# Position bias of an attention and mixture kernel: units decided on whole distances in float16, against knots computed once

## The chip, the cores and the metric

The kernel runs on one core of a Trainium2 chip. The metric is the time of one execution on the device, in microseconds (us). The engines of a core run side by side, each through its own list of instructions in order: TensorE (PE; PEld is its weight loads), VectorE (DVE), ScalarE (ACT), GpSimd (POOL), and SyncE (SP), which here issues DMA transfers. SBUF is the core's working memory, PSUM the memory into which TensorE's products go.

## The reference

Three blocks follow each other: an attention with a learned position bias (batch 2, 8 heads, 576 positions, 64 wide), a three-way max block, and eight experts over which a gate spreads 1152 tokens. The change is in the position bias alone:

```python
rel = (pos[:, None] - pos[None, :]).astype(np.float32)
psi_rel = np.log1p(np.abs(rel))
psi_i = np.log1p(np.maximum(pos[:, None].astype(np.float32), 1.0))
x = (psi_rel / psi_i)[..., None]
h = np.maximum(x @ w1 + b1, 0.0)        # 32 hidden units
bias = h @ w2                           # 8 heads
scores = scores + bias.transpose(2, 0, 1)[None, :, :, :]
```

A hidden unit d is active for row i and column j where w1[d] * psi_rel + b1[d] * psi_i is positive. Where it is active it adds w1[d] * w2[d, h] to a sum A and b1[d] * w2[d, h] to a sum B, and the bias is A * psi_rel / psi_i + B.

## The kernel before

The rows i are taken in 36 blocks of 16 (`g16`), and each block in four groups of 4 rows (`g`, 144 in all). For a group, `gen_s` makes a tile `s` of 128 partitions (4 rows by 32 units) and 576 columns that tells by sign which units are active. It compares a window of the table `lw` (logarithms of distances, times w1, float32), which moves by 4 columns from group to group, with a threshold per partition. ScalarE does this with a sign function (1 or -1) in 58 groups, VectorE with a comparison less one half (0.5 or -0.5, line 282) in 86; `ON_DVE` says which. Since these values are not 1 and 0, a constant is added back: A's in the bias of line 339, B's by a product of `cb` with `sel` (line 332).

`bias_mm` sums over the units on TensorE: for a block 32 products of 288 columns, with block-diagonal weights `wb` in two float16 parts, into PSUM tiles for A and for B; a 128-wide result holds 16 rows by 8 heads. `bias_ev` takes A out of PSUM on ScalarE (`t`, line 339) and multiplies it by the logarithms on GpSimd (line 342; on VectorE in the last two blocks, `LASTV`). `bias_out` joins it with B on VectorE (`bo`, line 347) and writes it to DRAM, from where the heads load it later.

The order is written out by hand. For each block come its products, `bias_ev`, the four `gen_s` of the block two later, and `bias_out`; in every other block GpSimd also prepares a sixth of a piece of the first head's operands (`prep_head`, lines 61 and 190). Buffers: 12 tiles `s`, 2 PSUM tiles each for A and B, 2 tiles `t`, 4 tiles `bo`. Ahead of the loop stand the loads of parameters (`par`) and tables, 12 products that nobody reads, and the weights' scaling on VectorE (lines 244 to 272). Behind the loop the attention starts with line 427 on VectorE and line 438 (exponentials) on ScalarE.

Of the kernel before, what the change touches and what calls it, by code (L numbers as in the profile page):

```python
# [27 lines left out]
SH = S // 2  # L28
# [14 lines left out]
ON_DVE = (0, 2, 4, 6, 8, 10, 11, 13, 14, 16, 18, 19)  # L43
ITS = [(0, 128), (128, 128), (256, 128), (384, 128), (512, 64)]

# [5 lines left out]
def make_body(stop=None):  # L51
    def body(tc, a):
# [21 lines left out]
        with ctx, tc.manual_schedule():  # L74
# [16 lines left out]
            def prep_w64(r, hi, lo):  # L91
                """A float64 weight tile [128, 512], made float32 on its bits and split, in steps."""
# [4 lines left out]
                # the exponent's floor is where float32's lowest exponent, and so 0, is made  # L97
# [25 lines left out]
            def w_step(n=1, last=99):  # L123
                """The next n steps of the weights' preparation, up to an item."""
# [15 lines left out]
            # ------------------------------------------------ operands of the heads  # L140
# [25 lines left out]
            def prep_head(h, k, part=None):  # L166
                """Operands of head h, piece k: hi, then what is left."""
# [34 lines left out]
            # ------------------------------------------------ position bias  # L202
            with ExitStack() as bctx:
# [5 lines left out]
                lw = bc.tile([128, L4_W], F32, name="lw")  # L209
                tab16 = bc.tile([128, L16_W + NG16], F32, name="tab16")  # L210
                dma(par, a["par"])
                # of the windows that slide over the logarithms, the first ones are the rightmost
                cuts = (0, 476, L4_W)
                nc.scalar.dma_start(out=lw[:, cuts[1]:], in_=a["tab4"][:, cuts[1]:])
                dma(lw[:, :cuts[1]], a["tab4"][:, :cuts[1]])
# [5 lines left out]
                # products that nobody reads, to have the tensor engine's clock up when the data are there  # L221
# [6 lines left out]
                half = bc.tile([32, 96], F32, name="half")  # L228
                G.memset(half, 0.5)
                sel = bc.tile([96, SH], BF16, name="sel")  # L230
                G.memset(sel, 0.0)
                for p in range(3):
                    G.memset(sel[32 * p:32 * p + 1], 1.0)
                bcv = bc.tile([128, NG4], F32, name="bcv")
                thr = bc.tile([128, NG4], F32, name="thr")
                pool_scale(bcv, c4, b1r)
                pool_copy(thr, bcv, -1.0)
                for sl in (slice(cuts[1], None), slice(0, cuts[1])):
                    A.activation(out=lw[:, sl], in_=lw[:, sl], func=AF.Identity, scale=w1r)
                # the power of two that brings the weights' largest product under 2^14, and its inverse  # L240
# [16 lines left out]
                # times 8, as the scores get their 1/8 with the bias in them  # L257
# [4 lines left out]
                # block-diagonal weights: [half-weights?, A or B, (i4, h)], in two float16 parts  # L262
                wf = bc.tile([128, 2, 2, 32], F32, name="wf")
                for q in range(2):
                    V.tensor_tensor(
                        out=wf[:, 0, q, :].rearrange("p (i h) -> p i h", h=H),
                        in0=ab[:, q, :].unsqueeze(1).to_broadcast([128, 4, H]),
                        in1=msk.rearrange("p (i h) -> p i h", h=H), op=ALU.mult)
                V.tensor_scalar(out=wf[:, 1], in0=wf[:, 0], scalar1=0.5, scalar2=None, op0=ALU.mult)
                wb = [bc.tile([128, 2, 2, 32], F16, name=f"wb{p}") for p in range(2)]  # L270
                V.tensor_copy(out=wb[0], in_=wf)
                V.tensor_tensor(out=wb[1], in0=wf, in1=wb[0], op=ALU.subtract)
                s_t = {}

                def gen_s(g):
                    s = sp.tile([128, S], F16, tag="s", name="s")
                    win = lw[:, L4_OFF - 4 * g:L4_OFF - 4 * g + S]
                    on_act = g % 20 not in ON_DVE
                    if on_act:
                        A.activation(out=s, in_=win, func=AF.Sign, bias=bcv[:, g:g + 1])  # L280
                    else:
                        V.tensor_scalar(out=s, in0=win, scalar1=thr[:, g:g + 1], scalar2=0.5,  # L282
                                        op0=ALU.is_gt, op1=ALU.subtract)
                    s_t[g] = s, int(on_act)
# [3 lines left out]
                # the constant part of the sums, by half-weights: A's with the row's logarithm, and B's as a  # L288
                # product of three bf16 parts (32 rows each) with ones in one row of each part
                ab16 = bc.tile([32, 2, 16, H], F32, name="ab16")  # L290
                for q in range(2):
                    G.tensor_copy(out=ab16[:, q], in_=ab[:32, q, :].unsqueeze(1).to_broadcast([32, 16, H]))
                cb = bc.tile([96, 128], BF16, name="cb")
                cr = bc.tile([96, 128], F32, name="cr")
                aic = bc.tile([128, 1 + 2 * NG16], F32, name="aic")
                a0, ia0, ics = aic[:, 0:1], aic[:, 1:1 + NG16], aic[:, 1 + NG16:]

                rows = ab16.rearrange("k q i h -> k q (i h)")
                T.matmul(out=p0[:, 0, 0:1], lhsT=rows[:, 0], rhs=half[:, 0:1], start=True, stop=True)
                T.matmul(out=p0[0:96, 0, 128:256], lhsT=half, rhs=rows[:, 1], start=True, stop=True)  # L300

                def consts():
                    V.tensor_scalar(out=ics, in0=ic16, scalar1=sc[:, 1:2], scalar2=None, op0=ALU.mult)
                    V.tensor_copy(out=a0, in_=p0[:, 0, 0:1])
                    V.tensor_scalar(out=ia0, in0=ics, scalar1=a0, scalar2=None, op0=ALU.mult)
                    b0 = p0[0:96, 0, 128:256]
                    V.tensor_copy(out=cb, in_=b0)
                    V.tensor_tensor(out=cr, in0=b0, in1=cb, op=ALU.subtract)
                    for p in (32, 64):
                        V.tensor_copy(out=cb[p:p + 32], in_=cr[p:p + 32])  # L310
                    V.tensor_tensor(out=cr[64:], in0=cr[64:], in1=cb[64:], op=ALU.subtract)
                    V.tensor_copy(out=cb[64:], in_=cr[64:])

                def bias_mm(g16):
                    ps = []
                    for q in range(2):
                        pt = pb[q].tile([128, 2, 512], F32, tag="p", name="p")
                        ps.append(pt)
                        for p in range(2):
                            for hf in range(2):  # L320
                                for c in range(4):
                                    s, on_act = s_t[4 * g16 + c]
                                    T.matmul(out=pt[32 * c:32 * c + 32, hf, :SH], lhsT=wb[p][:, on_act, q, :],  # L323
                                             rhs=s[:, hf * SH:hf * SH + SH], start=(p == 0), stop=(p == 1 and q == 0))
                    for c in range(4):
                        del s_t[4 * g16 + c]
                    if g16 == 0:
                        consts()
                        for g in range(4, 8):
                            gen_s(g)  # L330
                    for hf in range(2):
                        T.matmul(out=ps[1][:, hf, :SH], lhsT=cb, rhs=sel, start=False, stop=True)
                    return ps

                v3 = lambda x: x.rearrange("p (f n) -> p f n", f=2)

                def bias_ev(g16, ps):
                    t = ev.tile([128, S], F32, tag="t", name="t")
                    A.activation(out=v3(t), in_=ps[0][:, :, :SH], func=AF.Identity, bias=ia0[:, g16:g16 + 1],
                                 scale=ics[:, g16:g16 + 1])  # L340
# [4 lines left out]
                def bias_out(g16, ps, t):  # L345
                    bo = ev.tile([128, S], F32, tag="bo", name="bo", bufs=4)
                    V.scalar_tensor_tensor(out=v3(bo), in0=ps[1][:, :, :SH], scalar=sc[:, 1:2], in1=v3(t),
# [27 lines left out]
            # ------------------------------------------------ attention  # L375
# [8 lines left out]
            with ExitStack() as actx:  # L384
# [6 lines left out]
                # exponentials, transposed: columns (b, i) of i < 256, and of the rest; the last  # L391
                # chunk of j holds hi in its lower rows and lo in its upper ones
# [26 lines left out]
                def u_max(u):  # L419
# [3 lines left out]
                    if k == 0:  # L423
                        # by units: minus the maxima, and the sums with their reciprocals
# [25 lines left out]
                def r_tr(h):  # L450
                    """The sums' reciprocals, (b, i) along the row, beside the last unit's tail."""
# [3 lines left out]
                def r_out(h):  # L455
                    """The same in each of 64 rows, by way of DRAM."""
# [16 lines left out]
                def r_mm():  # L473
                    """The last head's, on all partitions by products with rows of the identity."""
# [17 lines left out]
                def u_trl(u):  # L492
                    """The last 64 columns; four units share a bank."""
# [11 lines left out]
                def u_ev(u):  # L505
                    """A unit's transposed tiles, split."""
# [592 lines left out]
```

## Time and profile before

| | us |
|---|---|
| three runs | 1177.23, 1179.74, 1180.08; median 1179.74 |
| span of the profiled execution | 1179.2 |
| TensorE busy in it | 1130.2 (96%) |
| VectorE busy | 744.1 (63%) |
| ScalarE busy | 513.9 (44%) |
| GpSimd busy | 381.2 (32%) |

The profile gives the profiled execution's own time as its span, from the first to the last instruction. Times of an instruction in it run from its start to its end; on VectorE and ScalarE the next instruction can start a little before the end, so the cost of one in a full queue is the distance from its start to the next start. In the views, "x3" is a count of like instructions merged into a row, and the brackets tell what ended the idle time before it. The granted clock is TensorE's, as a share of full speed (1.00 is 2.4 GHz, 0.50 is 1.2 GHz).

### The profile page before, as it was taken

How to read it: one execution, taken by the hardware profiler on the slowest of the kernel's cores; microseconds unless marked ns; L12 is line 12 of the kernel's file. 1: busy time of each engine (PE TensorE's matmuls, PEld its weight loads, DVE VectorE, ACT ScalarE, POOL GpSimd, SP SyncE). 2: the span in 40 equal slices, each digit the busy share in tenths (PEclk: the TensorE clock that was granted, in tenths of full speed). 3: DMA queues.
4: the chain of work that ended last, by engine and by line, in shares of the span. 5: the costliest groups of instructions: out<-in, count | busy, mean ns of one | idle time of the engine just before them, and what ended most of it. 6: DMA issues, size and time to landing. Idle time of an engine off the chain costs nothing.

```text
span 1179.2 us, 19134 instructions
## 1 busy us (share of the span) xinstructions
PE 1130.2 (96%) x7654; PEld 1003.9 (85%) x7654; DVE 744.1 (63%) x1221; ACT 513.9 (44%) x884; POOL 381.2 (32%) x316
## 2 busy tenths in 40 slices
PE   7776999999999999999999999999999999999998
PEld 3333888999999988889989899899898998998987
DVE  8999999977774476746456365464463553644623
ACT  6665898863432463415225134153251341532510
POOL 5668578912220450513113022031131220321310
PEclk8889999999999999999999999999999999999999
DMA  4353666403330021102012021021120110211102
GB/s 152 132 185 124 215 202 213 140 30 108 108 113 31 19 73 35 45 28 72 27 46 65 17 64 45 28 72 34 39 72 9 63 45 28 73 36 36 55 18 81
DMA packets 35432, 87.77 MB, mean 74 GB/s; under 512 B 5455, under 2 KB 5774, under 8 KB 34446
## 3 DMA queue, kind: packets, MB, share of 16 engines
q1 hardware_dynamic: 35198, 86.20, 22.4%
q8 instruction: 60, 0.98, 0.3%
q10 hardware_dynamic: 144, 0.34, 0.1%
q14 instruction: 30, 0.25, 0.1%
HBM read 73.52 MB, written 13.01 MB: 73 GB/s over the span
## 4 chain that ended last, share of the span: by engine, by line
PE 72%; DVE 13%; issue 3%; ACT 2%; DMA 0%; DVEq 0%; ACTq 0%
PE d L1011 33%; PE x L929 12%; PE z L929 8%; PE y L929 8%; PE o L807 3%; PE m L581 3%; DVE ng L427 3%; DVE ptl L503 2%; DVE ww L100 1%; DVE ww L105 1%; PE sc L410 1%; DVE ww L103 1%; PE pv L540 1%; DVE x L553 1%; ACT ww L99 1%
## 5 line engine op out<-in xcount | busy, mean ns | idle before, releaser
L1022 DVE SCALAR_TENSOR_TENSOR acc<-d,P,acc 128x512 f32<-128x512 f32 x135 | 101.4, 751 | 239.8 <-PE d L1011 239.7
L997 POOL TENSOR_TENSOR w2l<-w2r,w2h 128x512 fp32r<-128x512 f32 x64 | 93.8, 1466 | 468.9 <-ACT w2h L996 445.9
L1011 PE MATMUL d<-w2h,hh 128*128 128x512 f32 x576 | 224.9, 390 | 0.0
L1011 PE MATMUL d<-w2h,hl 128*128 128x512 f32 x576 | 224.7, 390 | 0.0
L1011 PE MATMUL d<-w2l,hh 128*128 128x512 f32 x576 | 224.4, 390 | 0.0
L937 ACT ACTIVATE s<-x 128x576 f32<-128x576 f32 x96 | 62.5, 651 | 355.8 <-PE x L929 352.6
L942 ACT ACTIVATE hh<-s 128x576 fp32r<-128x576 f32 x128 | 87.9, 687 | 93.4 <-DVE s L954 43.4
L1011 PEld LDWEIGHTS d<-w2h,hl 128*128 128x128 f32 x576 | 108.1, 188 | 23.0 <-DVE hl L947 0.3
L1011 PEld LDWEIGHTS d<-w2l,hh 128*128 128x128 f32 x576 | 108.1, 188 | 22.0
L1011 PEld LDWEIGHTS d<-w2h,hh 128*128 128x128 f32 x576 | 108.2, 188 | 21.9
L947 DVE SCALAR_TENSOR_TENSOR hl<-s,hh 128x576 fp32r<-128x576 f32 x128 | 103.1, 823 | 1.8 <-ACT hh L942 1.5
L323 PE MATMUL p<-s,wb 128*32 128x288 f16 x1152 | 62.4, 325 | 25.2 <-DVE s L282 23.2
L929 PE MATMUL x<-xth,w1h 128*128 128x288 f32 x384 | 82.6, 297 | 0.5 <-ACT acc L810 0.5
L747 POOL TENSOR_TENSOR w1l<-wf,w1h 128x768 fp32r<-128x768 f32 x32 | 59.2, 1851 | 72.4 <-ACT w1h L746 72.4
L929 PE MATMUL x<-xtl,w1h 128*128 128x288 f32 x384 | 82.3, 296 | 0.0
L929 PE MATMUL x<-xth,w1l 128*128 128x288 f32 x384 | 82.1, 295 | 0.0
L323 PEld LDWEIGHTS <-wb 128*32 128x32 f16 x1152 | 32.8, 105 | 53.2 <-issue 37.8
L282 DVE TENSOR_SCALAR s<-lw,thr 128x576 f16<-128x576 f32 x86 | 76.3, 934 | 0.0
L581 PE MATMUL m<-xh,wh 128*128 128x384 f32 x216 | 73.8, 341 | 2.1 <-DVE t L699 2.0
L581 PE MATMUL m<-xl,wh 128*128 128x384 f32 x216 | 73.1, 338 | 0.0
L581 PE MATMUL m<-xh,wl 128*128 128x384 f32 x216 | 73.1, 338 | 0.0
L963 DVE TENSOR_TENSOR s<-y,s 128x576 f32<-128x576 f32 x32 | 24.2, 757 | 73.2 <-ACT w1h L750 68.4
(193 smaller groups left out, 2601.2 us busy)
## 6 DMA issues: line engine op xcount, KB each, us to landing
wf<-in_moe_w SPq DMA_DIRECT2D x32, 512.0 KB, 3.5
w2r<-in_moe_w SPq DMA_DIRECT2D x64, 256.0 KB, 2.5
bias_d<-bo SPq DMA_DIRECT2D x36, 288.0 KB, 2.2
bias<-bias_d SPq DMA_DIRECT2D x32, 288.0 KB, 3.0
wr<-in_moe_w SPq DMA_DIRECT2D x18, 512.0 KB, 3.4
qk<-in_qk SPq DMA_DIRECT2D x7, 1152.0 KB, 7.2
wr<-in_moe_w_out SPq DMA_DIRECT2D x6, 512.0 KB, 3.5
vr<-in_v SPq DMA_DIRECT2D x8, 320.0 KB, 5.0
```

The lines of the kernel that those rows point to most:

```text
L282: V.tensor_scalar(out=s, in0=win, scalar1=thr[:, g:g + 1], scalar2=0.5, op0=ALU.is_gt, op1=ALU.subtract)
L323: T.matmul(out=pt[32 * c:32 * c + 32, hf, :SH], lhsT=wb[p][:, on_act, q, :], rhs=s[:, hf * SH:hf * SH + SH], start=(p == 0), stop=(p == 1 ...
L427: V.tensor_tensor_reduce(out=ng.rearrange("p (f n) -> p f n", f=2), in0=w["sc"][:, :, :SH], in1=bias_t[h, k // 2].rearrange("p (f n) -> p ...
L581: T.matmul(out=p[:, :TG], lhsT=ws[:, 128 * c:128 * c + 128], rhs=xs[:, c, TG * g:TG * g + TG], start=(c == 0 and n == 0), stop=(c == 3 and ...
L747: G.tensor_tensor(out=lo[:, 0:3], in0=t[:, 1:4], in1=raw(hi[:, 0:3]), op=ALU.subtract)
L929: T.matmul(out=ps[bank][:, s, :SH], lhsT=ws[:, i, c, :], rhs=xs[:, j, c, s * SH:s * SH + SH], start=(start and k == 0), stop=(k == 5), **kw)
L937: A.activation(out=t, in_=src, func=AF.Copy)
L942: A.activation(out=o, in_=src, func=AF.Relu)
L947: V.scalar_tensor_tensor(out=l, in0=src, scalar=0.0, in1=raw(o), op0=ALU.max, op1=ALU.subtract)
L997: G.tensor_tensor(out=lo, in0=r, in1=raw(hi), op=ALU.subtract)
L1011: T.matmul(out=pd, lhsT=hs[:, fh, 128 * t:128 * t + 128], rhs=ws, start=(k == 0), stop=(k == 11))
L1022: V.scalar_tensor_tensor(out=acc[:, t, :], in0=pd, scalar=P[:, t, e:e + 1], in1=acc[:, t, :], op0=ALU.mult, op1=ALU.add)
```

## The change

The activity of a unit is decided on the distance itself. From b1 and w1 a knot per partition and group, the distance at which the unit switches, is computed once on VectorE with an exponential by polynomial (`thr`; rounded to a half for ScalarE, `nthr`). The table is now the whole distances in float16 (`rr`), times the sign of w1 (`rs`). VectorE's compare gives 1 or 0 from float16 to float16; ScalarE gives the same by a steep sigmoid, in 53 groups, and VectorE has 91. A tile `s` is three rows of 192 columns at a pitch of 194. The constants that were added back, with their products, are gone. TensorE's 32 products of a block are of 384 and 192 columns. GpSimd's multiplication stays where it was.

```diff
-ON_DVE = (0, 2, 4, 6, 8, 10, 11, 13, 14, 16, 18, 19)
+STEEP = 256.0
+def on_act(g):
+    return g > 3 and g % 8 in (2, 5, 7)
...
-                cuts = (0, 476, L4_W)
-                nc.scalar.dma_start(out=lw[:, cuts[1]:], in_=a["tab4"][:, cuts[1]:])
-                dma(lw[:, :cuts[1]], a["tab4"][:, :cuts[1]])
+                nc.scalar.dma_start(out=rr, in_=a["tab4"])
...
-                pool_scale(bcv, c4, b1r)
-                pool_copy(thr, bcv, -1.0)
-                for sl in (slice(cuts[1], None), slice(0, cuts[1])):
-                    A.activation(out=lw[:, sl], in_=lw[:, sl], func=AF.Identity, scale=w1r)
+                def ts(out, in0, s1, o0, s2=None, o1=None):
+                    kw = {} if o1 is None else {"op1": o1}
+                    V.tensor_scalar(out=out, in0=in0, scalar1=s1, scalar2=s2, op0=o0, **kw)
+                MAGIC = 1.5 * 2.0 ** 23
+                ts(sg, w1r, 0.0, ALU.is_ge, 2.0, ALU.mult)
+                ts(sg, sg, -1.0, ALU.add)
+                ts(dn, w1r, sg, ALU.mult, 1e-30, ALU.max)
+                V.reciprocal(out=dn, in_=dn)
+                ts(kap, b1r, sg, ALU.mult, dn, ALU.mult)
+                ts(v, c4, kap, ALU.mult, -8.0, ALU.max)
+                ts(v, v, 8.0, ALU.min, -1.4426950408889634, ALU.mult)
+                ts(kf, v, MAGIC, ALU.add)
+                ts(kf, kf, -MAGIC, ALU.add)
+                V.tensor_tensor(out=f, in0=v, in1=kf, op=ALU.subtract)
+                ts(pw.bitcast(I32), kf, 127.0, ALU.add, 2.0 ** 23, ALU.mult)
+                taylor = [np.log(2.0) ** n / math.factorial(n) for n in range(8)]
+                ts(po, f, float(taylor[7]), ALU.mult)
+                for n in range(6, 0, -1):
+                    V.scalar_tensor_tensor(out=po, in0=po, scalar=float(taylor[n]), in1=f, op0=ALU.add, op1=ALU.mult)
+                V.scalar_tensor_tensor(out=po, in0=po, scalar=1.0, in1=pw, op0=ALU.add, op1=ALU.mult)
+                ts(thr, po, sg, ALU.mult, sg, ALU.subtract)
+                ts(rs, rr, sg, ALU.mult)
...
-                    s = sp.tile([128, S], F16, tag="s", name="s")
-                    win = lw[:, L4_OFF - 4 * g:L4_OFF - 4 * g + S]
-                    on_act = g % 20 not in ON_DVE
-                    if on_act:
-                        A.activation(out=s, in_=win, func=AF.Sign, bias=bcv[:, g:g + 1])
+                    s = sp.tile([128, 3, 194], F16, tag="s", name="s")[:, :, :192]
+                    win = rs[:, L4_OFF - 4 * g:L4_OFF - 4 * g + S]
+                    if on_act(g):
+                        A.activation(out=s, in_=win.rearrange("p (a b) -> p a b", a=3), func=AF.Sigmoid, bias=nthr[:, g:g + 1], scale=STEEP)
                     else:
-                        V.tensor_scalar(out=s, in0=win, scalar1=thr[:, g:g + 1], scalar2=0.5,
-                                        op0=ALU.is_gt, op1=ALU.subtract)
+                        V.tensor_scalar(out=s, in0=win.rearrange("p (a b) -> p a b", a=3), scalar1=thr[:, g:g + 1],
+                                        scalar2=None, op0=ALU.is_gt)
...
-                def consts():
-                    V.tensor_scalar(out=ics, in0=ic16, scalar1=sc[:, 1:2], scalar2=None, op0=ALU.mult)
...
+                ts(po, po, -1.5, ALU.add, MAGIC, ALU.add)
+                ts(po, po, -MAGIC, ALU.add, 0.5, ALU.add)
+                ts(nthr, po, sg, ALU.mult, -STEEP, ALU.mult)
+                for g in range(4, 8):
+                    gen_s(g)
+                V.tensor_scalar(out=ics, in0=ic16, scalar1=sc[:, 1:2], scalar2=None, op0=ALU.mult)
...
-                            for hf in range(2):
+                            for sl in (slice(0, 2), slice(2, 3)):
                                 for c in range(4):
-                                    s, on_act = s_t[4 * g16 + c]
-                                    T.matmul(out=pt[32 * c:32 * c + 32, hf, :SH], lhsT=wb[p][:, on_act, q, :],
-                                             rhs=s[:, hf * SH:hf * SH + SH], start=(p == 0), stop=(p == 1 and q == 0))
+                                    T.matmul(out=thirds(pt)[32 * c:32 * c + 32, sl, :], lhsT=wb[p][:, q, :],
+                                             rhs=s_t[4 * g16 + c][:, sl, :], start=(p == 0), stop=(p == 1))
...
-                    for hf in range(2):
-                        T.matmul(out=ps[1][:, hf, :SH], lhsT=cb, rhs=sel, start=False, stop=True)
...
-                    A.activation(out=v3(t), in_=ps[0][:, :, :SH], func=AF.Identity, bias=ia0[:, g16:g16 + 1],
-                                 scale=ics[:, g16:g16 + 1])
+                    A.activation(out=v3(t), in_=thirds(ps[0]), func=AF.Copy, scale=ics[:, g16:g16 + 1])
...
-    l4 = psi(np.arange(L4_W)[None, :] - L4_OFF - (p // 32)[:, None])
+    l4 = np.abs(np.arange(L4_W)[None, :] - L4_OFF - (p // 32)[:, None]).astype(np.float16)
```

VectorE at the start, from the weights (`wf`, `wb`) to the first blocks, before the change (`cb`, `cr` and `aic` are the constants):

```order
L272 TENSOR_TENSOR wb_171<-wf,wb_170 128x128
L282 TENSOR_SCALAR s<-lw,thr 128x576 x2
L303 TENSOR_SCALAR aic<-tab_113,sc 128x36
L304 COPY aic<-p_125 128x1
L305 TENSOR_SCALAR aic<-aic 128x36
L307 CAST cb<-p_125 96x128
L308 TENSOR_TENSOR cr<-p_125,cb 96x128
L310 CAST cb<-cr 32x128 x2
L311 TENSOR_TENSOR cr<-cr,cb 32x128
L312 CAST cb<-cr 32x128
L282 TENSOR_SCALAR s<-lw,thr 128x576 x5
L347 SCALAR_TENSOR_TENSOR bo<-p,sc,t 128x576
```

The same engine after the change, first ahead of the weights (`one` holds the one-column values, `eu` the knots on their way, `big` is the first of the weights' scaling):

```order
L236 TENSOR_SCALAR eu<-par,one 128x144
L236 TENSOR_SCALAR eu<-eu 128x144 x3
L256 TENSOR_TENSOR eu<-eu 128x144
L236 TENSOR_SCALAR eu<-eu 128x144 x2
L261 SCALAR_TENSOR_TENSOR eu<-eu 128x144 x6
L262 SCALAR_TENSOR_TENSOR eu<-eu 128x144
L236 TENSOR_SCALAR thr<-eu,one 128x144
L236 TENSOR_SCALAR rs<-rr,one 128x1148
L269 TENSOR_REDUCE big<-par 128x32
```

and then from the weights to the first blocks:

```order
L296 TENSOR_TENSOR wb_182<-wf,wb_181 128x64
L307 TENSOR_SCALAR s<-rs,thr 128x3x192 x4
L236 TENSOR_SCALAR eu<-eu 128x144 x2
L236 TENSOR_SCALAR nthr<-eu,one 128x144
L307 TENSOR_SCALAR s<-rs,thr 128x3x192 x2
L319 TENSOR_SCALAR ics<-tab_113,sc 128x36
L307 TENSOR_SCALAR s<-rs,thr 128x3x192 x3
L350 SCALAR_TENSOR_TENSOR bo<-p,sc,t 128x576
```

The knots' instructions now stand ahead of everything else on VectorE, and the constants' instructions, which stood between the compares, are gone.

On ScalarE, the end of the stage after the change, where the stage's last activations meet the attention's first (`pe` are the exponentials):

```order
L343 ACTIVATE t<-p,ics 128x576
L305 ACTIVATE s<-rs,nthr 128x3x192 x2
L343 ACTIVATE t<-p,ics 128x576 x2
L104 ACTIVATE ww<-wr 128x512
L441 ACT_TABLE_LOAD
L441 ACTIVATE pe,st<-ng,st 128x576 x2
```

There was no table load at this place before; a second one stands ahead of the first sigmoid, at line 305.

## Rows read from the trace of the kernel before

**Rows 1.** Chain of waits, first 116 us: start us, us, what.

```profile
114.39 0.82 DVE bo L347
115.21 0.66 DVE ng L427
```

**Rows 2.** Busy time in a stretch: stretch, length, engines busy (instructions), clock, DMA, GB/s.

```profile
12.89:115.21 102.32, 74.72 (x1199) 36.92 (x1198) 102.14 (x122) 64.50 (x89) 72.00 (x59) 0.88 0.39 136
```

**Rows 3.** Groups of instructions, 9 to 115 us: VectorE's compare; busy us, mean ns.

```profile
L282 DVE TENSOR_SCALAR s<-lw,thr 128x576 f16<-128x576 f32 x85 | 75.9, 939 | 0.0
```

**Rows 4.** Two lines by themselves: ns of one, min/median/max, first and last start.

```profile
L282 DVE TENSOR_SCALAR s<-lw,thr x86: 502/881/1735, 8.1 to 107.4; 128x576 f16<-128x576 f32 x86
...
L347 DVE SCALAR_TENSOR_TENSOR bo<-p,sc,t x36: 797/805/818, 14.4 to 114.4; 128x576 f32<-128x576 f32 x36
```

**Rows 5.** VectorE in order of time, mid-stage: start us, us, instruction.

```profile
31.19 0.93 DVE L282 TENSOR_SCALAR s<-lw,thr 128x576 f16<-128x576 f32 x2
32.05 0.80 DVE L347 SCALAR_TENSOR_TENSOR bo<-p,sc,t 128x576 f32<-128x576 f32 x1
32.77 3.64 DVE L282 TENSOR_SCALAR s<-lw,thr 128x576 f16<-128x576 f32 x3
```

**Rows 6.** GpSimd in order of time, start and mid-stage.

```profile
10.77 1.40 POOL L342 TENSOR_TENSOR t<-t,tab 128x576 f32<-128x576 f32 x1 [3.18 <-ACT t L339]
15.37 1.56 POOL L342 TENSOR_TENSOR t<-t,tab 128x576 f32<-128x576 f32 x1 [3.21 <-ACT t L339]
...
32.27 1.42 POOL L342 TENSOR_TENSOR t<-t,tab 128x576 f32<-128x576 f32 x1 [2.05 <-ACT t L339]
33.65 0.89 POOL L61 TENSOR_SCALAR qs<-qk 128x576 fp32r<-128x576 f32 x1
34.50 1.59 POOL L342 TENSOR_TENSOR t<-t,tab 128x576 f32<-128x576 f32 x1
```

**Rows 7.** VectorE in order of time, the start of the kernel.

```profile
4.82 0.42 DVE L244 TENSOR_REDUCE big<-par 128x32 f32<-128x256 f32 x1 [3.43 <-DMA par<-in_par]
...
5.85 0.15 DVE L250 TENSOR_SCALAR big<-big 128x1 f32<-128x1 f32 x1
6.04 0.15 DVE L251 TENSOR_SCALAR sc<-big 128x1 int32<-128x1 int32 x1
...
7.68 0.23 DVE L271 CAST wb<-wf 128x128 f16<-128x128 f32 x1
7.94 0.29 DVE L272 TENSOR_TENSOR wb<-wf,wb 128x128 f16<-128x128 f32 x1
8.15 0.94 DVE L282 TENSOR_SCALAR s<-lw,thr 128x576 f16<-128x576 f32 x2
...
10.93 1.31 DVE L312 CAST cb<-cr 32x128 bf16<-32x128 f32 x1
12.28 2.24 DVE L282 TENSOR_SCALAR s<-lw,thr 128x576 f16<-128x576 f32 x5
```

**Rows 8.** VectorE in order of time, the stage's end: the multiplication of the last blocks.

```profile
109.69 1.99 DVE L342 TENSOR_TENSOR t<-t,tab 128x576 f32<-128x576 f32 x1
```

**Rows 9.** ScalarE in order of time, mid-stage.

```profile
33.00 0.83 ACT L339 ACTIVATE t<-p,aic 128x576 f32<-128x576 f32 x1
33.73 1.43 ACT L280 ACTIVATE s<-lw,bcv 128x576 f16<-128x576 f32 x2
```

**Rows 10.** TensorE in order of time, mid-stage: the 32 products of two blocks.

```profile
38.87 1.98 PE L323 MATMUL p<-s,wb 128*32 128x288 f16 x32
...
41.13 1.17 PE L323 MATMUL p<-s,wb 128*32 128x288 f16 x32
```

**Rows 11.** ScalarE in order of time: the first table load, and the first exponential.

```profile
1.17 1.28 ACT L224 ACT_TABLE_LOAD   x1 [1.17 <-PEq L1089]
...
115.92 0.78 ACT L438 ACTIVATE pe<-ng,st 128x576 f32<-128x576 f32 x1 [4.67 <-DVE st L427]
```

**Rows 12.** Busy time in the densest quarter of the stage, columns as in rows 2.

```profile
65.00:90.00 25.00, 19.59 (x339) 9.60 (x339) 25.00 (x34) 17.77 (x26) 17.79 (x15) 0.93 0.58 202
```

More of the change, by code (lines that the diff above doesn't have):

```diff
@@ L1 @@
+import math
 from contextlib import ExitStack
@@ L208, in body @@
                 par = bc.tile([128, 2 + H + 32 + NG4 + 2 * HID + HID * H], F32, name="par")
-                lw = bc.tile([128, L4_W], F32, name="lw")
+                rr = bc.tile([128, L4_W], F16, name="rr")
                 tab16 = bc.tile([128, L16_W + NG16], F32, name="tab16")
                 dma(par, a["par"])
-                cuts = (0, 476, L4_W)
-                nc.scalar.dma_start(out=lw[:, cuts[1]:], in_=a["tab4"][:, cuts[1]:])
-                dma(lw[:, :cuts[1]], a["tab4"][:, :cuts[1]])
+                nc.scalar.dma_start(out=rr, in_=a["tab4"])
                 dma(tab16, a["tab16"])
@@ L227, in body @@
                     T.matmul(out=p0[:, 1, :], lhsT=wz[:, :128], rhs=wz, start=True, stop=True)
[L228 to L234, printed above, removed]
-                thr = bc.tile([128, NG4], F32, name="thr")
@@ new lines, in body @@
+                one = bc.tile([128, 4], F32, name="one")
+                sg, kap, dn = one[:, 0:1], one[:, 1:2], one[:, 2:3]
+                eu = bc.tile([128, 5, NG4], F32, name="eu")
+                v, kf, f, po, pw = (eu[:, i] for i in range(5))
+                thr = bc.tile([128, NG4], F32, name="thr")
+                nthr = bc.tile([128, NG4], F32, name="nthr")
+                rs = bc.tile([128, L4_W], F16, name="rs")
+                ts(sg, w1r, 0.0, ALU.is_ge, 2.0, ALU.mult)
+                ts(sg, sg, -1.0, ALU.add)
@@ L261, in body @@
                 V.tensor_scalar(out=ab, in0=ab, scalar1=sc[:, 0:1], scalar2=None, op0=ALU.mult)
-                wf = bc.tile([128, 2, 2, 32], F32, name="wf")
+                wf = bc.tile([128, 2, 32], F32, name="wf")
                 for q in range(2):
                     V.tensor_tensor(
-                        out=wf[:, 0, q, :].rearrange("p (i h) -> p i h", h=H),
+                        out=wf[:, q, :].rearrange("p (i h) -> p i h", h=H),
                         in0=ab[:, q, :].unsqueeze(1).to_broadcast([128, 4, H]),
@@ L268, in body @@
                         in1=msk.rearrange("p (i h) -> p i h", h=H), op=ALU.mult)
-                V.tensor_scalar(out=wf[:, 1], in0=wf[:, 0], scalar1=0.5, scalar2=None, op0=ALU.mult)
-                wb = [bc.tile([128, 2, 2, 32], F16, name=f"wb{p}") for p in range(2)]
+                wb = [bc.tile([128, 2, 32], F16, name=f"wb{p}") for p in range(2)]
                 V.tensor_copy(out=wb[0], in_=wf)
                 V.tensor_tensor(out=wb[1], in0=wf, in1=wb[0], op=ALU.subtract)
+                ics = bc.tile([128, NG16], F32, name="ics")
@@ L284, in gen_s @@
-                    s_t[g] = s, int(on_act)
+                    s = sp.tile([128, 3, 194], F16, tag="s", name="s")[:, :, :192]
+                    win = rs[:, L4_OFF - 4 * g:L4_OFF - 4 * g + S]
+                    if on_act(g):
+                        A.activation(out=s, in_=win.rearrange("p (a b) -> p a b", a=3), func=AF.Sigmoid, bias=nthr[:, g:g + 1], scale=STEEP)
+                    else:
+                        V.tensor_scalar(out=s, in0=win.rearrange("p (a b) -> p a b", a=3), scalar1=thr[:, g:g + 1],
+                                        scalar2=None, op0=ALU.is_gt)
@@ L286, in body @@
+                    s_t[g] = s
                 for g in range(4):
                     gen_s(g)
[L290 to L296, printed above, removed]
@@ L298, in body @@
-                rows = ab16.rearrange("k q i h -> k q (i h)")
-                T.matmul(out=p0[:, 0, 0:1], lhsT=rows[:, 0], rhs=half[:, 0:1], start=True, stop=True)
-                T.matmul(out=p0[0:96, 0, 128:256], lhsT=half, rhs=rows[:, 1], start=True, stop=True)
-                def consts():
-                    V.tensor_scalar(out=ics, in0=ic16, scalar1=sc[:, 1:2], scalar2=None, op0=ALU.mult)
[L304 to L312, printed above, removed]
+                ts(po, po, -1.5, ALU.add, MAGIC, ALU.add)
@@ L314, in bias_mm, with thirds @@
+                ts(po, po, -MAGIC, ALU.add, 0.5, ALU.add)
[3 more added lines that the diff above has]
+                V.tensor_scalar(out=ics, in0=ic16, scalar1=sc[:, 1:2], scalar2=None, op0=ALU.mult)
+                def thirds(pt):
+                    return pt.rearrange("p a (b n) -> p (a b) n", b=2)[:, 0:3, :192]
                 def bias_mm(g16):
@@ L319, in bias_mm @@
                         for p in range(2):
-                            for hf in range(2):
+                            for sl in (slice(0, 2), slice(2, 3)):
                                 for c in range(4):
-                                    s, on_act = s_t[4 * g16 + c]
-                                    T.matmul(out=pt[32 * c:32 * c + 32, hf, :SH], lhsT=wb[p][:, on_act, q, :],
-                                             rhs=s[:, hf * SH:hf * SH + SH], start=(p == 0), stop=(p == 1 and q == 0))
+                                    T.matmul(out=thirds(pt)[32 * c:32 * c + 32, sl, :], lhsT=wb[p][:, q, :],
+                                             rhs=s_t[4 * g16 + c][:, sl, :], start=(p == 0), stop=(p == 1))
                     for c in range(4):
                         del s_t[4 * g16 + c]
[L327 to L330, printed above, removed]
-                    for hf in range(2):
-                        T.matmul(out=ps[1][:, hf, :SH], lhsT=cb, rhs=sel, start=False, stop=True)
                     return ps
-                v3 = lambda x: x.rearrange("p (f n) -> p f n", f=2)
+                v3 = lambda x: x.rearrange("p (f n) -> p f n", f=3)
                 def bias_ev(g16, ps):
                     t = ev.tile([128, S], F32, tag="t", name="t")
-                    A.activation(out=v3(t), in_=ps[0][:, :, :SH], func=AF.Identity, bias=ia0[:, g16:g16 + 1],
-                                 scale=ics[:, g16:g16 + 1])
+                    A.activation(out=v3(t), in_=thirds(ps[0]), func=AF.Copy, scale=ics[:, g16:g16 + 1])
                     eng = G if g16 < NG16 - LASTV else V
@@ L346, in bias_out @@
                     bo = ev.tile([128, S], F32, tag="bo", name="bo", bufs=4)
-                    V.scalar_tensor_tensor(out=v3(bo), in0=ps[1][:, :, :SH], scalar=sc[:, 1:2], in1=v3(t),
+                    V.scalar_tensor_tensor(out=v3(bo), in0=thirds(ps[1]), scalar=sc[:, 1:2], in1=v3(t),
                                            op0=ALU.mult, op1=ALU.add)
```

## The prediction

> **What bounds the kernel now.** I first asked the chain of waits for the opening 116 us. It is a single engine: the last `bo` ends at 115.21 us and the first attention instruction of VectorE begins there [rows 1]. The busy times of that stretch say the same: from 12.89 to 115.21 us VectorE is busy for 102.14 of 102.32 us, with TensorE at 74.72, GpSimd at 72.00 and ScalarE at 64.50 [rows 2]. So the position bias is a VectorE stage, and what VectorE saves there the end saves, until another engine of the stage is full. Everything behind the stage is the same instructions in the same order.
>
> Next I asked the groups of instructions what VectorE does. 85 compares at L282 are 75.9 us, 939 ns each [rows 3]. But their own line gives 502 to 1735 ns [rows 4], a wide spread for one shape. The other large VectorE instruction, `bo` at L347, always takes 797 to 818 ns. VectorE in order of time explains it [rows 5]: two compares together take 0.93 us, and soon after three take 3.64 us. GpSimd's list beside it [rows 6] shows why: while the two ran (31.19 to 32.12) GpSimd waited, and while the three ran (32.77 to 36.41) it multiplied and copied. The clearest single case is a 32x128 cast that begins at 10.93 us and ends at 12.24, 70 ns behind a GpSimd multiplication that ran from 10.77 to 12.17; five compares right after it, before GpSimd's next instruction at 15.37, take 2.24 us [rows 6, 7]. So a compare costs 0.86/2 = 0.43 us from start to start (31.19 to 32.05) when GpSimd is quiet, and otherwise stands until GpSimd's instruction ends. `bo` never does: it costs 0.72 us from start to start (32.05 to 32.77) whatever GpSimd does.
>
> **The change, part by part.** I keep VectorE's ledger from 4.82 us, where its parameters have landed [rows 7], since before the change it never idles from there on.
>
> New work ahead of the weights: 5 one-column instructions, each fed by the last, at 6.04 - 5.85 = 0.19 us, 0.95 us; 7 plain instructions on 144 columns (the knots' `v`, `kf`, `pw`, `po`, `thr`), nearest row the 128-column cast with 0.26 us to the next start, 1.8 us; 8 with two tensors, nearest row 0.29 us, 2.4 us; one pass over the 1148 float16 distances, between 0.43 us (the price of 576) and twice that, 0.6 us. That is 5.8 us, all in series, with nothing beside it. The weights' own chain stays: 8.15 - 4.82 = 3.3 us.
>
> The compares: 91 instead of 86 (ScalarE has 53 instead of 58). No float16-to-float16 compare is in the trace. From above: `bo`'s 0.72 us, and with GpSimd in the way the old 0.9. From below: if `bo` goes through its 576 columns at half the pace of the undisturbed compare, the 0.29 us between them leave 0.14 us fixed, and twice the compare's pace would be 0.14 + 0.145 = 0.28 us. I take 0.43 us, the undisturbed compare, and no standing behind GpSimd. My reading of the rows: what stands are the instructions that take 4-byte data at twice `bo`'s pace, or two tensors of SBUF (1.99 us at L342, [rows 8]), and so must work on two places of it at once; `bo`, with one such tensor at half that pace, never stands. With 2-byte data two elements can come from one place. And the built program gives the new compare one row of 576 as source and three rows of 192 that do not join as destination, which can't be cut into like halves. 91 x 0.43 = 39.1 us.
>
> The Trainium skill (Vector Engine (DVE) Microarchitecture Reference, section on performance modes) states that an instruction with one source uses both ports only if the outermost counts of source and destination are both even, or equal; 576 against 3 is neither, so by it the compare gets two elements per cycle from pairs of 16-bit values and leaves the second port alone. The skill (SBUF — State Buffer, section Who interferes with whom) has GpSimd and VectorE share only that second pair, as an exclusive lock; the trace agrees for the old compares [rows 6, 7]. By both the sum is the one I use. Without the padding the same rules would make it a two-port instruction.
>
> The rest: `bo`, 36 x 0.72 = 25.9 us, unchanged; two multiplications on VectorE near the end, 2 x 1.99 = 4.0 us at the old price [rows 8], as GpSimd still works beside them; the three instructions for ScalarE's knots and `ics`, 1.0 us. Gone are the constants' eight instructions between the first compares' end at 9.09 us and 12.28, 3.2 us [rows 7], and TensorE's L332 products; on TensorE I cost their removal at nothing, as it waits there.
>
> Sum: 5.8 + 3.3 + 39.1 + 25.9 + 4.0 + 1.0 = 79.1 us, so VectorE could end at 83.9 us if it never waited.
>
> **What is late next.** By pairs of row blocks (five compares and two `bo` on VectorE, three activations and two `t` on ScalarE): VectorE 5 x 0.43 + 2 x 0.72 = 3.6 us; GpSimd two multiplications at 1.40 us and a head's operand piece at 0.89 [rows 6], 3.7 us; ScalarE two `t` at 0.73 us (33.00 to 33.73) and three activations at about 0.7 (two in 1.43), 3.6 us [rows 9]; TensorE at the full clock 2 x 1.17, at the half clock 2 x 1.98 = 4.0 us [rows 10]. The ring from `bo` to the `t` that reuses its buffer, GpSimd's multiplication and the next `bo` but one is 0.83 + 1.41 + 0.81 us and three hand-overs of 0.1 us, 3.35 us. So all come within 0.3 us of each other: the old stage had 102.3/35 x 2 = 5.8 us per pair. In-order queues this full do not mesh without loss. I add 1.5 us for the first block (its products, `t` and multiplication stand in series ahead of the first `bo`) and 0.15 us for each of 17 pairs, 2.5 us. VectorE then ends at 83.9 + 4.0 = 87.9 us in place of 115.2: 27.3 us less.
>
> Costed at nothing: the second and third table load on ScalarE (1.28 us each, [rows 11]). The one for the sigmoid runs while ScalarE waits for the knots; the one for the exponentials falls into the 4.67 us that ScalarE idles before its first exponential. With that cover gone each is 1.3 us. The SP queue keeps its order less one load. Its writes come closer: the densest quarter moved 202 GB/s at a DMA share of 0.58 [rows 12], and at 1.6 times the pace that is 0.93, near full. Four `bo` buffers absorb some of it; if not, a few us.
>
> The profiled execution's span is 1179.2 us, 0.5 us under the median of the runs, 1179.7. 1179.7 - 27.3 = 1152.4 us.
>
> **Rivals.**
> 1. The lock stays (slower). If the new compare still stands behind GpSimd, VectorE pays what it paid: start to start about 0.89 us (75.9/85). Then the ledger is 5 x 0.89 for more compares, 5.8 for the knots and 1.0 for the small ones, less 3.2 us: +8.1 us, 1187.8 us. It decides from a compare of 0.80 us on, where 91 x 0.80 and the longer start equal the old 86 x 0.89. For it: every fast VectorE instruction of this stage with both sides in SBUF shows it. Against: the shape of the two sides, and that `bo`, which has only one operand there, never stands. By the skill (VectorE: DVE Perf Modes, tier table) this operation at 16 bits in SBUF takes the two-port mode of four per cycle, which is the lock's case; it bears here only if like halves are not asked for.
> 2. `bo`'s pace: the unlike sides cost the pairing as well. 0.72 us, no standing. A pair of blocks is then 7 x 0.72 = 5.0 us on VectorE, the ledger 79.1 + 91 x 0.29 = 105.5 and some 2 us of waits, an end at 112.3: 2.9 us less, 1176.8 us. Against: the half pace of 4-byte data is what one place gives, and 2-byte data need half of it.
> 3. TensorE on the half clock. The granted clock was 0.93 in the densest quarter [rows 12], and groups at half pace are in the trace [rows 10]. TensorE will also stand idle behind its warm-up products until the knots are made. Were it at half speed throughout, a pair costs 4.0 us and more: 17 x 0.5 = 8 us back, 1160.5 us. Against: less idle time per pair than now, when it was granted most of full speed.
> 4. The queues mesh worse, or DMA lags: 0.5 us more per pair, 1161 us.
>
> **How the numbers follow.** The forecast, 1147 to 1158 us around 1152.4, has 0.62; rivals 3 and 4 together 0.19, both still faster; rival 2 0.07; rival 1 0.08; the remaining 0.04 is a faster compare that only GpSimd's 3.7 us limits, 1148 us. The range of 8 in 10 is 1146 to 1170 us: it holds the forecast, rivals 3 and 4 and a compare up to 0.62 us (91 x 0.19 = 17 us). A change under 0.3%, 3.5 us, can't be told from none. Faster 0.85, the same 0.07 (rival 2's 2.9 us), slower 0.08.
>
> **What would show it.** The compares should lie close together, near 0.45 us, also under GpSimd's multiplications; if they spread again up to 1.7 us, rival 1 holds; at a flat 0.75 us, rival 2. The first compare should begin near 14 us, and the last `bo` end near 88. GpSimd's multiplication should stay at 1.40 us. VectorE should no longer be busy throughout: its waits should be short and for GpSimd's `t`, and GpSimd be busy for some 62 of 72 us. TensorE's groups of 32 products at 1.2 us say the full clock, at 2.0 the half. The forecast is wrong if the stage's gain is given back behind it, by a first exponential or a head's operands that are late.

## The result

| | before | after |
|---|---|---|
| median of the runs | 1179.38 us | 1151.2 us |
| runs | 1177.23 to 1180.08 (4) | 1150.27 to 1152.07 (4) |
| span of the profiled execution | 1179.2 us | 1148.5 us |

The ratio is 0.9765, 95% interval 0.9752 to 0.9779: the change makes the kernel 2.35% faster, 28.2 us. The forecast was 1152.4 us.

The stage's busy times, in the form of [rows 2]: the stretch, its length, then TensorE, TensorE's loads, VectorE, ScalarE and GpSimd, the granted clock, the DMA share and GB/s.

```profile
20.00:80.00 60.00, 55.26 (x1072) 27.73 (x1071) 59.80 (x117) 56.47 (x84) 58.14 (x53) 1.00 0.65 222
...
60.00:80.00 20.00, 18.65 (x368) 9.31 (x362) 20.00 (x39) 18.37 (x29) 18.88 (x20) 1.00 0.74 251
...
60.00:70.00 10.00, 9.36 (x187) 4.69 (x185) 10.00 (x21) 9.51 (x16) 9.54 (x10) 1.00 0.93 310
...
9.00:18.00 9.00, 3.98 (x47) 2.73 (x51) 8.54 (x34) 2.10 (x4) 0.00 (x0) 0.50 0.00 0
```

VectorE is still busy all the time, but now the other three are close to it: GpSimd stands at 58.14 of 60 us, where it had 72.00 of 102.32 [rows 2]. TensorE's clock is full from 20 us on; at the start, where TensorE stands idle until 13.92 us, it is 0.50 from 9 to 18 us. Over 20 us the DMA share does not pass 0.74, but over the 10 us from 60 to 70 it is 0.93, and VectorE is busy for all of them.

The two lines of [rows 4], with ScalarE's `t` beside them (ns of one, min/median/max, first and last start):

```profile
L307 DVE TENSOR_SCALAR s<-rs,thr x91: 496/506/518, 13.4 to 77.9; 128x576 f16<-128x576 f16 x91
```

```profile
L350 DVE SCALAR_TENSOR_TENSOR bo<-p,sc,t x36: 802/811/823, 19.5 to 82.2; 128x576 f32<-128x576 f32 x36
```

```profile
L343 ACT ACTIVATE t<-p,ics x36: 721/741/743, 17.3 to 79.2; 128x576 f32<-128x576 f32 x36
```

The compare's spread of 502 to 1735 ns is gone: the slowest of 91 takes 518. The same stretch in order of time, VectorE and then GpSimd, in the form of [rows 5, 6]:

```profile
39.81 1.34 DVE L307 TENSOR_SCALAR s<-rs,thr 128x576 f16<-128x576 f16 x3
41.26 0.82 DVE L350 SCALAR_TENSOR_TENSOR bo<-p,sc,t 128x576 f32<-128x576 f32 x1
41.99 0.93 DVE L307 TENSOR_SCALAR s<-rs,thr 128x576 f16<-128x576 f16 x2
42.83 0.81 DVE L350 SCALAR_TENSOR_TENSOR bo<-p,sc,t 128x576 f32<-128x576 f32 x1
```

```profile
39.81 2.79 POOL L345 TENSOR_TENSOR t<-t,tab 128x576 f32<-128x576 f32 x2
42.57 0.68 POOL L66 TENSOR_SCALAR kh<-qk 128x576 fp32r<-128x576 f32 x1
43.21 2.80 POOL L345 TENSOR_TENSOR t<-t,tab 128x576 f32<-128x576 f32 x2
```

GpSimd multiplies from 39.81 to 42.60 without a pause, and VectorE's five compares in that time and just behind it take their 0.42 us each (41.99 to 42.83 for two) all the same.

The start and the end of the stage on VectorE, as in [rows 7, 8, 1]:

```profile
4.47 0.15 DVE L236 TENSOR_SCALAR one<-par 128x1 f32<-128x1 f32 x1 [3.08 <-DMA par<-in_par]
...
7.38 2.02 DVE L261 SCALAR_TENSOR_TENSOR eu<-eu 128x144 f32<-128x144 f32 x6
...
10.48 0.41 DVE L269 TENSOR_REDUCE big<-par 128x32 f32<-128x256 f32 x1
...
13.36 1.77 DVE L307 TENSOR_SCALAR s<-rs,thr 128x576 f16<-128x576 f16 x4
...
19.51 0.82 DVE L350 SCALAR_TENSOR_TENSOR bo<-p,sc,t 128x576 f32<-128x576 f32 x1 [1.39 <-POOL t L345]
```

```profile
79.07 1.09 DVE L345 TENSOR_TENSOR t<-t,tab 128x576 f32<-128x576 f32 x1
80.25 0.82 DVE L350 SCALAR_TENSOR_TENSOR bo<-p,sc,t 128x576 f32<-128x576 f32 x1
80.98 1.08 DVE L345 TENSOR_TENSOR t<-t,tab 128x576 f32<-128x576 f32 x1
82.15 0.82 DVE L350 SCALAR_TENSOR_TENSOR bo<-p,sc,t 128x576 f32<-128x576 f32 x1
82.89 0.75 DVE L430 CUSTOM_DVE_ANT_0 ng<-sc,bias 128x576 f32<-128x576 f32 x1
```

The last `bo` ends at 82.97 us, 32.2 us earlier than before [rows 1], and the attention begins at once. The table load for the exponentials, as in [rows 11], ends at 81.84 us inside ScalarE's wait:

```profile
80.56 1.28 ACT L441 ACT_TABLE_LOAD   x1
83.68 0.78 ACT L441 ACTIVATE pe<-ng,st 128x576 f32<-128x576 f32 x1 [1.83 <-DVE st L430]
```

### The profile page after: what moved, and what is told of

It reads as the page before. It is cut to its first block, busy times and chain, and to the rows that moved or that the text cites. A ratio compares the mean times of both kernels' runs of the same rounds, so it can differ in the third digit from the quotient of the medians.

```text
span 1148.5 us, 18982 instructions
## 1 busy us (share of the span) xinstructions
PE 1115.9 (97%) x7578; PEld 999.8 (87%) x7578; DVE 711.9 (62%) x1241; ACT 506.7 (44%) x879; POOL 373.3 (33%) x307
## 4 chain that ended last, share of the span: by engine, by line
PE 70%; DVE 16%; issue 4%; ACT 2%; DMA 1%; DVEq 0%; ACTq 0%; SPq 0%
PE d L1014 34%; PE x L932 11%; PE y L932 8%; PE z L932 8%; PE o L810 3%; DVE ng L430 3%; DVE ptl L506 3%; PE m L584 2%; DVE ww L105 1%; DVE ww L108 1%; DVE ww L110 1%; DVE pth L506 1%; DVE x L556 1%; DMA wf<-in_moe_w 1%; ACT ww L104 1%
## 5 line engine op out<-in xcount | busy, mean ns | idle before, releaser
L945 ACT ACTIVATE hh<-s 128x576 fp32r<-128x576 f32 x128 | 87.9, 687 | 95.6 <-DVE s L957 46.3
L750 POOL TENSOR_TENSOR w1l<-wf,w1h 128x768 fp32r<-128x768 f32 x32 | 59.3, 1853 | 76.6 <-ACT w1h L749 76.6
L333 PE MATMUL p<-s,wb 128*32 128x192 f16 (+1 forms) x1152 | 60.9, 295 | 13.1 <-DVE s L307 8.0
L932 PEld LDWEIGHTS x<-xth,w1h 128*128 128x128 f32 x384 | 62.5, 188 | 2.0 <-ACT acc L813 0.7
```

What stands on the lines that cost most here:

```text
L333: T.matmul(out=thirds(pt)[32 * c:32 * c + 32, sl, :], lhsT=wb[p][:, q, :], rhs=s_t[4 * g16 + c][:, sl, :], start=(p == 0), stop=(p == 1))
L750: G.tensor_tensor(out=lo[:, 0:3], in0=t[:, 1:4], in1=raw(hi[:, 0:3]), op=ALU.subtract)
L932: T.matmul(out=ps[bank][:, s, :SH], lhsT=ws[:, i, c, :], rhs=xs[:, j, c, s * SH:s * SH + SH], start=(start and k == 0), stop=(k == 5), **kw)
L945: A.activation(out=o, in_=src, func=AF.Relu)
```

## The experiments

The theory is that of the prediction: the unlike sides keep the compare clear of GpSimd, the 16-bit data give it its pace, and neither does the work of the other. The first four kernels are the changed kernel with one or both taken back.

**Padding undone.**

```diff
-s = sp.tile([128, 3, 194], F16, tag="s", name="s")[:, :, :192]
+s = sp.tile([128, 3, 192], F16, tag="s", name="s")
```

> The changed kernel with the padding alone undone: float16 distances, and a tile of 576 columns without gaps. Theory (like halves): the compare's two sides can now be cut alike, so it goes at twice the padded compare's pace, some 0.28 us from start to start where GpSimd is quiet, but it stands behind GpSimd again: single compares from 0.3 to 1.7 us, GpSimd and VectorE take turns, a pair of blocks costs about 4.5 to 5.2 us in place of 3.55, and the time is 1168 to 1185 us. Rival (16-bit data): float16 alone frees the compare from GpSimd and the padding does nothing; then compares are a flat 0.28 to 0.45 us and the time is 1148 to 1152 us.

Measured: 1174.13 us, ratio to before 0.9963 (0.9948 to 0.9979). The compare by itself, and VectorE and GpSimd in order of time:

```profile
L307 DVE TENSOR_SCALAR s<-rs,thr x91: 352/555/1574, 13.3 to 100.4; 128x576 f16<-128x576 f16 x91
```

```profile
39.90 0.64 DVE L307 TENSOR_SCALAR s<-rs,thr 128x576 f16<-128x576 f16 x2
40.45 0.81 DVE L350 SCALAR_TENSOR_TENSOR bo<-p,sc,t 128x576 f32<-128x576 f32 x1
41.18 3.64 DVE L307 TENSOR_SCALAR s<-rs,thr 128x576 f16<-128x576 f16 x3
```

```profile
40.95 2.83 POOL L345 TENSOR_TENSOR t<-t,tab 128x576 f32<-128x576 f32 x2 [1.00 <-ACT t L343]
43.86 0.79 POOL L195 TENSOR_TENSOR qs<-qk,qs 64x288 fp32r<-64x288 f32 x1
```

With GpSimd quiet two compares take 0.55 us from start to start, 0.28 each, the faster pace. With two multiplications and a subtraction running on GpSimd, three take 3.64 us, as long as in [rows 5]. The faster instruction makes the slower kernel: 23 us are lost by filling two gaps in a tile.

**Two rows in place of three.**

```diff
-s = sp.tile([128, 3, 194], F16, tag="s", name="s")[:, :, :192]
+s = sp.tile([128, 2, 290], F16, tag="s", name="s")[:, :, :288]
...
```

(with TensorE's products and the results in PSUM at 288 columns).

> The changed kernel with the tile as two rows of 288 columns at a pitch of 290 in place of three of 192 at 194, and TensorE's products at 288 columns as before the change. The rows still don't join, but two rows and 576 elements can both be halved. Theory (like halves): the compare stands behind GpSimd again, 0.3 to 1.7 us, as without padding, and the time is 1168 to 1185 us. Rival (any gap is enough): the compare is a flat 0.5 us and the time is 1150 to 1153 us.

Measured, one run: 1175.02 us.

```profile
L307 DVE TENSOR_SCALAR s<-rs,thr x91: 354/558/1576, 13.6 to 100.9; 128x576 f16<-128x576 f16 x91
```

This gap does nothing: the line reads as without padding. So a gap is not what keeps GpSimd and VectorE apart; three rows against 576 elements do, and two rows don't. The rule of the Trainium skill (Vector Engine (DVE) Microarchitecture Reference, section on performance modes), outermost counts both even or equal, sorts these two and the padded kernel as the runs do.

**Float32 distances, padding kept.**

```diff
-rs = bc.tile([128, L4_W], F16, name="rs")
+rs = bc.tile([128, L4_W], F32, name="rs")
```

(likewise `rr` and the table).

> The changed kernel with the distances in float32 and the padding kept. Theory: the padding keeps the compare away from GpSimd, and float16 gives the pace; so the compare is a flat 0.73 us from start to start (0.8 us long), never standing; a pair of blocks costs VectorE 7 x 0.73 = 5.1 us and the time is 1151 + 17.5 x 1.5 = 1177 us. Rival (4-byte compares always stand): spread from 0.5 to 1.7 us, mean 0.9, 1185 us or more. Rival (float16 does nothing): a flat 0.43 us and 1151 us.

Measured: 1178.39 us, ratio to before 0.9997 (0.9988 to 1.0007).

```profile
L307 DVE TENSOR_SCALAR s<-rs,thr x91: 801/810/818, 14.9 to 104.8; 128x576 f16<-128x576 f32 x91
```

```profile
43.47 1.53 DVE L307 TENSOR_SCALAR s<-rs,thr 128x576 f16<-128x576 f32 x2
44.91 0.82 DVE L350 SCALAR_TENSOR_TENSOR bo<-p,sc,t 128x576 f32<-128x576 f32 x1
```

It never stands, and it goes at `bo`'s pace: 0.72 us from start to start (43.47 to 44.91 for two). This is the prediction's second rival in the flesh: 1176.8 us were worked out for it.

**Both undone.** The edits of the first and the third together.

> The changed kernel with float32 distances and without padding: only the knots, the 1 and 0 and the missing constants are left of the change. Theory: the compare is that of the kernel before, 0.43 us from start to start or standing behind GpSimd, mean 0.9 us, and the time is the rival's sum of the prediction less the half of a compare's second operation: 1182 to 1190 us. Rival (the gain lies in the constants and their products): 1150 to 1165 us.

Measured, one run: 1188.83 us.

```profile
L307 DVE TENSOR_SCALAR s<-rs,thr x91: 502/514/1712, 14.5 to 113.0; 128x576 f16<-128x576 f32 x91
```

```profile
L307 DVE TENSOR_SCALAR s<-rs,thr 128x576 f16<-128x576 f32 x91 | 76.6, 889 | 0.0
```

```profile
120.01 0.82 DVE L350 SCALAR_TENSOR_TENSOR bo<-p,sc,t 128x576 f32<-128x576 f32 x1
```

The compare stands as in [rows 4]: its spread is the same and its sum 76.6 us (75.9 in [rows 3]), though more of the 91 than of the old 86 go undisturbed (median 514 ns, before 881). The kernel is about 10 us slower than before: this is the first rival, 1187.8 us. What remains of the change, the knots ahead of the weights and five more compares against the constants saved, costs time. But the last `bo` ends at 120.83 us, 5.6 us later than before, where the rival had 8.1; the rest lies behind the stage or between the runs. Together, with 1188.8 from a single run:

| us | dense | three padded rows |
|---|---|---|
| float32 | 1188.8 | 1178.4 |
| float16 | 1174.1 | 1151.2 |

Padding alone gives 10 us and float16 alone 15; both give 38, since a pace that only holds while GpSimd is quiet, or freedom at half the pace, each leave VectorE the longest.

**TensorE's products put back.** Two per block, with zeros in `cb`, so that the sums stay.

```diff
+for sl in (slice(0, 2), slice(2, 3)):
+    T.matmul(out=thirds(ps[1])[:, sl, :], lhsT=cb, rhs=sel[:, sl, :], start=False, stop=True)
...
```

(the sums are now closed by these products, and GpSimd sets `cb` and `sel` at the start).

> The changed kernel with the removed products of TensorE put back, two per block (384 and 192 columns) with a matrix of zeros, so that the sums stay as they are. The prediction costed their removal at nothing. Theory A (TensorE still has room: 1.17 + 0.42 = 1.6 us per block against 1.78): under 1 us, 1150 to 1152 us. Theory B (the stage is so full that the ring through PSUM feels them): 0.1 to 0.42 us per block, 1155 to 1166 us.

Measured: 1148.78 us, ratio to before 0.9756 (0.9743 to 0.977), which overlaps the change's own interval.

```profile
20.00:80.00 60.00, 58.05 (x1139) 29.06 (x1139) 59.80 (x117) 55.95 (x84) 58.11 (x53) 1.00 0.65 222
```

TensorE goes from 55.26 to 58.05 us and VectorE's 59.80 do not move. Costing these products at nothing was right; by busy time TensorE still has 2 us of 60 to spare.

**The multiplication on VectorE.** The other way out of the lock: take GpSimd away.

```diff
-LASTV = 2
+LASTV = NG16
```

and the dense tile.

> The changed kernel without padding and with the multiplication of all blocks on VectorE in place of GpSimd, which then has only the head's operands: the lock is avoided by taking GpSimd away instead. Theory: compares near 0.28 us with few standing, a pair of blocks on VectorE 5 x 0.28 + 2 x 0.73 for bo + 2 x 0.7 for the multiplications = 4.3 us and up to 0.3 of standing, against 3.55 with the multiplication on GpSimd: 1163 to 1172 us. Rival (the lock costs so much that VectorE alone is as good): 1148 to 1155 us.

Measured, one run: 1169.91 us.

```profile
17.15 2.47 DVE L307 TENSOR_SCALAR s<-rs,thr 128x576 f16<-128x576 f16 x4
...
42.09 0.75 DVE L345 TENSOR_TENSOR t<-t,tab 128x576 f32<-128x576 f32 x1
42.76 0.64 DVE L307 TENSOR_SCALAR s<-rs,thr 128x576 f16<-128x576 f16 x2
43.32 0.81 DVE L350 SCALAR_TENSOR_TENSOR bo<-p,sc,t 128x576 f32<-128x576 f32 x1
...
47.50 0.81 DVE L350 SCALAR_TENSOR_TENSOR bo<-p,sc,t 128x576 f32<-128x576 f32 x1
```

With GpSimd idle the compare is at its 0.28 us, but each block now has 0.67 us of multiplication on the engine that bounds the stage (42.09 to 42.76), and a pair of blocks takes 4.18 us (43.32 to 47.50), against 3.56 in the changed kernel. The standing is not wholly gone: GpSimd now prepares the head's operands without the multiplications in between, most of them from 8.93 to 22.20 us and from 63.00 to 73.75, and VectorE stands behind it there. The first compare begins at 17.15 us and not at 13.36, and single compares still take up to 1.57 us. With the dense tile the multiplication on VectorE is some 4 us the better (1169.9 against 1174.1 us), from a single run. GpSimd's multiplication earns its place only if the compare does not stand behind it.

**A version that beats both.** The new start is in series; the exponential of the knots is moved to ScalarE, which idles there, and VectorE goes on with the weights.

```diff
-ts(v, v, 8.0, ALU.min, -1.4426950408889634, ALU.mult)
-ts(kf, v, MAGIC, ALU.add)
...
-V.scalar_tensor_tensor(out=po, in0=po, scalar=1.0, in1=pw, op0=ALU.add, op1=ALU.mult)
+ts(v, v, 8.0, ALU.min)
+A.activation(out=po, in_=v, func=AF.Exp, scale=-1.0)
```

(`thr` and `nthr` come behind the weights).

> The changed kernel with the knots' exponential as one ScalarE activation in place of the polynomial of 13 VectorE instructions, which ran from 6.2 to 9.8 us with TensorE, ScalarE and GpSimd idle; meanwhile VectorE goes on with the weights' chain, and ScalarE's knots are made ahead of the first compare. Theory (the start is in series and all of it counts): the first compare begins near 10.3 us in place of 13.36, the first bo some 4 us earlier, and the time is 1147 to 1148 us. Rival (the stage behind it, where GpSimd and VectorE are both full, or DMA at a share of 0.74, absorbs it): less than 1 us, 1150.5 us or more.

Measured: 1145.9 us, ratio to before 0.972 (0.9705 to 0.9734), below the change's interval. ScalarE and VectorE at the start, and the last `bo`:

```profile
6.29 0.32 ACT L254 ACTIVATE eu<-eu 128x144 f32<-128x144 f32 x1 [3.52 <-DVE eu L236]
6.63 1.28 ACT L300 ACT_TABLE_LOAD   x1
10.74 1.44 ACT L300 ACTIVATE s<-rs,nthr 128x576 f16<-128x576 f16 x2 [2.82 <-DVE nthr L236]
```

```profile
10.62 2.61 DVE L302 TENSOR_SCALAR s<-rs,thr 128x576 f16<-128x576 f16 x6
...
15.87 0.82 DVE L342 SCALAR_TENSOR_TENSOR bo<-p,sc,t 128x576 f32<-128x576 f32 x1 [1.23 <-POOL t L337]
...
78.68 0.82 DVE L342 SCALAR_TENSOR_TENSOR bo<-p,sc,t 128x576 f32<-128x576 f32 x1
```

The first compare begins 2.7 us earlier and the first `bo` 3.6, with ScalarE's first sigmoids 5.2 us earlier (10.74 us, where the changed kernel has 15.90). The last `bo` ends at 79.50, 3.5 us earlier: the full stage behind the start absorbs next to nothing. The medians differ by more than the traces (5.3 against 3.5 us at the stage's end, and 2.7 in span); runs of one kernel spread over 2 to 5 us, and the intervals allow all of these.

## Why the prediction was right, step by step

- **The compare** was the step on which all hung. Taken: 0.43 us, no standing; measured 0.42 and a spread of 22 ns. The four kernels show both halves of the reason apart, and the bounds were real: 0.28 us dense (worked out as 0.28), 0.72 us in float32 (taken from `bo`), 0.5 to 1.7 us with the lock.
- **The start.** 5.8 us for the knots and distances: 10.48 - 4.47 = 6.0. The weights' chain 3.3 us: 2.9, as one instruction left and the two behind it were halved. First compare at 13.36 us, expected near 14.
- **The end.** The two multiplications on VectorE were costed at 2 x 1.99; from start to the next `bo` they took 2 x 1.18 = 2.4 us. The 1.99 us were mostly standing, behind a subtraction on GpSimd that began with it before:

```profile
109.65 1.41 POOL L190 TENSOR_TENSOR qs<-qk,qs 64x576 fp32r<-64x576 f32 x1
```

  It ended 0.62 us behind that subtraction (111.68 against 111.06). Both multiplications still end 0.6 us behind an instruction of GpSimd, but that one now ends sooner after their start (at 79.55 and 81.44 us, see the last section).
- **What is late next.** The period came out as VectorE's own: 41.26 to 44.82 us, 3.56 us, forecast 3.6. GpSimd's sum was a little too large: 3.40 us (39.81 to 43.21), forecast 3.7. The loss by meshing was the term most mis-sized: 2.5 us were added for 17 pairs, but VectorE idles 0.2 us in 60. So the sign that VectorE would no longer be busy throughout did not come. ScalarE's `t` had become shorter (741 in place of 830 ns [rows 9]; a copy with one scale stands in place of an identity with scale and bias); that this is why `t` was seldom late is not shown. The first block's wait was 1.39 us, 1.5 taken.
- **Sum.** VectorE ended at 82.97 us, not 87.9, and 32.2 us were saved at that point, not 27.3. Of the 4.9 us between them the meshing is 2.5 and the end 1.6. That the time still agrees within 1.2 us is partly luck. The span fell by 30.7 us, so 1.5 us were given back behind the stage. In the chain of waits of the changed kernel two late loads stand among the experts, start us, us and what:

```profile
647.64 3.71 DMA wf<-in_moe_w
1071.17 5.01 DMA wf<-in_moe_w
```

  No such row was in the chain of before, and their place is 560 us and more behind the change. The shorter stage is not their cause: the chain of the kernel with both undone, whose stage ends later than before, has three such rows, this the longest:

```profile
1109.18 5.62 DMA wf<-in_moe_w
```

  What makes them late stays open. The other 2.5 us lie between profile and medians: each run of the changed kernel is 1.8 us above its span, so the profiled execution of before, were it the same there, was some 1.6 us slower than its median, and that of after is 0.9 us under its own. The forecast had set the profile's span against the median as if nothing lay between.
- **The rivals.** TensorE on the half clock: no, 1.00 from 20 to 80 us, and 0.50 only behind its idle time at the start. DMA: the share that was scaled to 0.93 stayed at 0.74 or below over 20 us and reached 0.93 over 10 (60 to 70), where VectorE was busy all the same. The lock and `bo`'s pace did not come, and both had their price right to 2 us when they were brought about. At the stage's end they were dearer in the sums than in the traces (110.86 us for `bo`'s pace, worked out as 112.3; 5.6 us for the lock in place of 8.1), so part of that agreement is luck too.

The largest part of the saving thus came from one pair of properties of a single instruction, 38 us, against 10 us that the rest of the change costs.

## What to carry to other kernels

When one shape of a VectorE instruction shows a wide spread of times, lay GpSimd's list beside it before counting its work; the fastest form of an instruction can be the slower choice if it must wait for a neighbour. A form with half the pace that never waits, got here by cutting the tile into three rows, was worth 23 us. And work left in series ahead of a full stage counted in full here: moving it to an idle engine brought the stage's end 3.5 us forward.

## What was not expected of the hardware

- The standing goes both ways. VectorE multiplies two SBUF tensors from 79.07 to 80.16 us and from 80.98 to 82.06. GpSimd's subtraction that begins at 79.63, beside the first, takes 1.81 us where its like takes 1.40. VectorE's second multiplication then stands behind that subtraction and ends 0.62 us after it:

```profile
78.89 0.66 POOL L66 TENSOR_SCALAR qs<-qk 128x576 fp32r<-128x576 f32 x1
79.63 1.81 POOL L195 TENSOR_TENSOR qs<-qk,qs 64x576 fp32r<-64x576 f32 x1
...
82.68 1.40 POOL L195 TENSOR_TENSOR qs<-qk,qs 64x576 fp32r<-64x576 f32 x1
```

- Three forms of the same 576-column compare to float16 cost 0.28 us (dense, from float16), 0.42 us (three rows, from float16) and 0.72 us (three rows, from float32) from start to start. An estimate: if each goes at half the pace of the one ahead of it, the steps of 0.14 and 0.30 us leave 0.12 to 0.14 us of each that does not depend on the columns.
